# Second weight pair rescaled two slots later, queries of two head pairs in one buffer, operand places and load order of the weights changed

## The chip, the cores and the metric

One core of one Trainium2 chip runs the whole program. The metric is device time in microseconds, the median of several executions. Each of them is one launch of a fused chain: pooled attention, a gated feed-forward layer, and a second gated feed-forward layer.

## The reference

```
k_p, v_p = mean of k, v over each 8 rows                  # 8 x 8 heads, 576 rows -> 72, 64 wide
a = softmax(q k_p^T / 8) v_p                              # x: [4608, 512]
h = x @ w_in;  g = h * clip(h + 3, 0, 6) / 6;  y = g @ w_out          # d_ff 2048
out = (silu(y @ w_gate) * (y @ w_val)) @ w_out2                       # d_ff 1536
```

All of it is float32. The kernel keeps float32 accuracy with float32r matmuls in threes: each operand is split into a high and a low part, and high*high, high*low and low*high are added up in PSUM. The weights come as raw 64-bit words and are converted to float32 on the chip.

## The kernel before, in words

The kernel has three stages, one after the other.

**First stage: attention and the first up-projection.** The 4608 rows are cut into NB = 9 blocks of N = 512. For block j, 16 up-projections (`up`, line 623: 12 matmuls of 512 columns each) run on TensorE, while the attention steps of block j + 1 are woven between them (`attn_slot`). A planner sorts the attention steps of all units by hand-set lags (`when`, `when_startup`); each engine executes its instructions in that order. A block's rows belong to one batch or to two, so that each head pair gives a *segment* of n rows per batch. Block 0 has n = 512, block 1 has 64 and 448, block 2 has 128 and 384, then 192/320, 256/256, 320/192, 384/128, 448/64, and 512 again. A segment's queries are fetched by four DMAs on SP's queue (line 384), 128 bytes a packet, into one of three buffers `q_in`; a VectorE transpose (line 485) turns them into `qT` for the scores (line 503). A load is issued 12 steps after the transpose of the third segment before it.

Beside this, in blocks 1 to 8 a *prep* converts the other weights. The list `prep_at` gives each of 26 preps its slots: a prep starts every 6 slots (one slot is one up-projection) and, from the 21st prep on, every 8 slots of the second stage. Its steps: fetch the first pair of quarters (slot 0) and the second pair (slot 1) into `wstg`; rescale both pairs on ScalarE (slot 3, line 135); join the 64-bit words of each pair on VectorE (slots 4 and 5, lines 141 and 144); sums (slot 7, on GpSimd, line 207 and 212); split into high and low part (slots 8 to 10); store to DRAM (slots 10 and 11).

**Second stage: the first down-projection**, in 9 blocks of 256-column products by Winograd's form of Strassen's scheme: 7 products per block (`down_b`, line 902), each of four chunks c = 0..3 of 12 matmuls, in the order c = 0, 1, 2, 3. The stationary operand is the weight chunk `pw`, the moving one the split activation `gb`. The weights of all seven products are fetched once from DRAM: those of products 0 to 2 late in the first stage, those of products 3 to 6 in a row right after its last stores of `g` (line 642), 16 loads of 512 KB (line 868).

**Third stage: the second layer**, in six groups p of 768 rows: 24 up-products in units of 7 (`up2`: P1, P6, P5, P2, P4, P7, P3, six matmuls of 384 columns each) and 7 down-products (`down2`, 54 matmuls of 256 columns each), all by line 716.

**Operand places.** Three tables shift where an operand starts inside its buffer, in 4-byte words: `P1_AT` for the four weight chunks of product 0 in the second stage (all other `pw` chunks start at multiples of 1024 in their buffers); `GC_AT` for the split activations of single chunks (n, c) in `down2`; and `X_AT` for the operands of `up2`, by name, with 8 where nothing is given.

All DMAs of these stages are issued by SP's queue in program order.

Of the kernel before, what the change touches and what calls it, by code (L numbers as in the profile page):

```python
# [23 lines left out]
def kernel(  # L24
# [27 lines left out]
    nc = tc.nc  # L52
# [174 lines left out]
    PREP_A = 20  # L227
    for u in range(len(preps)):
        first = 6 * u if u < PREP_A else F1 * (NB - 1) + 6 + 8 * (u - PREP_A)
        for step, off in enumerate((0, 3, 4, 5, 7, 8, 9, 9, 10, 10, 11, 1)):  # L230
            prep_at.setdefault(first + off, []).append((u, step))

    def prep_slot(n):
# [4 lines left out]
    def prep_step(u, step):  # L238
        kind, f, m = preps[u]
        if step in (0, 11):  # L240
            place = A7 if kind == "up" else B7
            pairs = (("11", "21"), ("12", "22")) if kind == "up" else (("11", "21"), ("22", "12"))
            for pair in pairs[step == 11:][:1]:
                t = stg_p.tile([P, WC, 2], F32, tag="stg", name="wstg")
                for i, quarter in enumerate(pair):
                    r, c = int(quarter[0]) - 1, int(quarter[1]) - 1
                    if kind == "up":
                        w = (w_gate, w_val)[m].bitcast(I32).rearrange("(k p) f -> p k f", p=P)
                        src = w[:, 2 * c:2 * c + 2, 2 * P * (2 * f + r):2 * P * (2 * f + r + 1)]
                    else:  # L250
                        row = P * (2 * f + r if kind == "dn" else NP1 * r + f)
                        w = (w_out2 if kind == "dn" else w_out).bitcast(I32)[row:row + P, :]
                        src = w[:, 4 * P * c:4 * P * (c + 1)]
                    fetch_into(t[:, WH * i:WH * (i + 1)], src)
                a, b = (place[quarter] for quarter in pair)
                prep_t.setdefault(("q", u), []).append((t, slice(a, b + 1, b - a)))
        elif step == 1:
            for s, _ in prep_t["q", u]:
                rescale(s)
        elif step in (2, 3):  # L260
            if step == 2:
                prep_t["f", u] = f32(new_q7("q7")).rearrange("p (s n) -> p s n", s=8)
            s, at = prep_t["q", u].pop(0)
            join(s, prep_t["f", u][:, at].bitcast(I32), 2)
        elif step == 4:
            q, eng = prep_t["f", u], nc.gpsimd if u < PREP_A else nc.vector
            if kind == "up":
                sums_a(eng, lambda n: q[:, A7[n]])
            else:
                sums_b(eng, lambda n: q[:, B7[n]])  # L270
        elif step in (5, 6):
            if step == 5:
                prep_t["s", u] = new_s7("s7").rearrange("p (s a n) -> p s a n", s=7, a=2)
            q, t, part = prep_t["f", u], prep_t["s", u], slice(0, 4) if step == 5 else slice(4, 7)
            nc.scalar.copy(out=t[:, part, 0], in_=q[:, part])
        elif step in (7, 8):
            q, t, part = prep_t["f", u], prep_t["s", u], slice(0, 4) if step == 7 else slice(4, 7)
            nc.vector.tensor_tensor(out=t[:, part, 1], in0=q[:, part], in1=f32(t[:, part, 0]), op=ALU.subtract)
        else:
            part = slice(0, 4) if step == 9 else slice(4, 7)  # L280
            t = prep_t["s", u][:, part]
            if kind == "up":
                nc.sync.dma_start(
                    out=s_up[f][m][:, part].rearrange("p s a k f -> p (s a k f)"),
                    in_=f32(t).rearrange("p s a f -> p (s a f)"),
                )
            else:
                nc.sync.dma_start(out=(s_dn if kind == "dn" else s_w1)[:, part, f], in_=f32(t))
# [23 lines left out]
    sync4 = [nc.sync] * 4  # L312

    def load_k(b, p, eng):
        t = a_p.tile([SP_, 2, POOL, D], F32, tag="k", name="k_in", bufs=2)
# [55 lines left out]
                    )  # L371
            vt_t[0, p] = vt[p // 2][:96, p % 2]

    def load_q(seg, engines):
        t = a_p.tile([P, N // 32, 32], F32, tag="q", name="q_in", bufs=3)
        fetch_q(t, seg, engines)
        q_t[seg] = t

    def fetch_q(t, seg, engines):
        b, p, s0, n = seg  # L380
        for h2 in range(2):
            for dh in range(2):
                p0 = 64 * h2 + 32 * dh
                engines[2 * h2 + dh].dma_start(  # L384
                    out=t[p0:p0 + 32, :n // 32],
                    in_=q[b, 2 * p + h2, s0:s0 + n, 32 * dh:32 * dh + 32]
                    .rearrange("(c s) d -> s c d", s=32),
                )

    def reduce_k(b, p):  # L390
        kp = a_p.tile([SP_, 2, D], F32, tag="kp", name="kp", bufs=2)
# [79 lines left out]
            op0=ALU.mult, op1=ALU.subtract,  # L471
        )

    def prep_q(seg):
        n = seg[3]
        t = a_p.tile([P, N // 32, 32], F32, tag="qT", name="qT", bufs=2)
        if seg in segs[:KT]:

            s, ps = q_t.pop(seg), psum("k", [P, QJ, P])
            for j in range(QJ):  # L480
                nc.tensor.transpose(out=ps[:, j], in_=s[:, j].rearrange("p h d -> p (h d)"), identity=ident)
            qT_t[seg] = t.rearrange("p c s -> p (c s)")
            nc.vector.tensor_copy(out=qT_t[seg].rearrange("d (p j) -> d j p", j=QJ), in_=ps)
            return
        nc.vector.transpose(out=t[:, :n // 32], in_=q_t.pop(seg)[:, :n // 32])  # L485
        qT_t[seg] = t.rearrange("p c s -> p (c s)")

    n_unit = [0]
    s_t, ps_t, x_ps, x_e, n_exp = {}, {}, {}, {}, [0]
# [173 lines left out]
            nc.sync.dma_start(out=t[:, 2 * r + c], in_=y_d[:, 2 * r:2 * r + 2, t0:t0 + M])  # L663
        ys[p] = t

    GC_AT = {(0, 0): 16, (3, 0): 56, (4, 0): 16}
    X_AT = {'21': 24, 'T3': 16}

    def x_step(p, n, lo_eng, sum_eng):

# [9 lines left out]
        a = X_AT.get(what, 8)  # L680
        x = xc[p, what] = x[:, a:a + 4 * M].rearrange("p (a k n) -> p a k n", a=2, k=2)
        split(x[:, 0], x[:, 1], v(what), lo_eng)
        if then:
# [171 lines left out]
            t = gq[j, slot] = lb["gq"].tile([P, NP1, MB], F32, tag=f"gq{slot}", name="gq")  # L855
            nc.sync.dma_start(out=t, in_=g_d[j][:, r, c])

    P1_AT = (16, 1088, 2168, 3216)

    def new_pw(n, t):  # L860
        k = BIG // NCB
        at = P1_AT if n == 0 else [k * c for c in range(NCB)]
        lb["pw", DN[n][2]] = [t[:, a:a + k].rearrange("p (f a n) -> p f a n", f=CB, a=2) for a in at]

    def load_pw(n, half):
        what = DN[n][2]
        for c in range(NCB // 2 * half, NCB // 2 * (half + 1)):
# [40 lines left out]
    def evac_b(j, n):  # L908
# [35 lines left out]
        elif what == "P3":  # L944
# [6 lines left out]
    units, unit_end, segs, heads = [], [], [], []  # L951
    seg_of, first_in_seg, first_in_head = {}, {}, {}
    for j in range(NB):
        t0 = j * N
        while t0 < (j + 1) * N:
# [5 lines left out]
            for p in range(KT):  # L961
                seg = (b, p, s0, n)
                at_unit = len(units) if alone or p % 2 == 0 else len(units) - 1
                first_in_seg.setdefault(at_unit, []).append(len(segs))
                segs.append(seg)
                if s0 == 0:
                    first_in_head.setdefault(at_unit, []).append(len(heads))
# [54 lines left out]


    at = {st: n for n, st in enumerate(steps)}
    seg_no = {sg: n for n, sg in enumerate(segs)}
    head_no = {hd: n for n, hd in enumerate(heads)}
    rings = {}

# [5 lines left out]

    for i, u in enumerate(units):
        before(*((what, i) for what in "SXANMEFTULVWY"))
    for i, sg in ((i, seg_no[s]) for i, u in enumerate(units) for s in seg_of[u]):
# [14 lines left out]
    for i, u in enumerate(units):  # L1052
# [17 lines left out]
    for sg, s in enumerate(segs):  # L1070
        ring("qT", 2, ("P", sg), ("S", max(i for i, u in enumerate(units) if s in seg_of[u])))
# [19 lines left out]
    def do_step(st):  # L1091
# [17 lines left out]
        elif what == "Q":  # L1109
            split_v_lo(*heads[i])  # L1110
        elif what == "P":
            prep_q(segs[i])
            for n in (range(KT, KT + 3) if i == KT - 1 else (i + 3,)):
                if KT <= n < len(segs) and i >= KT - 1:
                    later.append((done[0] + 12, lambda n=n: load_q(segs[n], sync4)))
        elif what == "S":
            scores(units[i])
        elif what == "N":
# [37 lines left out]
    with tc.manual_schedule():  # L1156
# [64 lines left out]
        for j in range(NB):  # L1221
            for f in range(F1):
                if (j, f) == (NB - 1, 0):
                    attn_ctx.close()
                    for nm in ("px", "gq"):
                        lb[nm] = right_b.enter_context(
                            tc.tile_pool(name=nm, bufs=1, side="right", reuse_waits="tile"))
                    new_pw(0, lb["px"].tile([P, 4296], F32R, tag="px", name="pw"))
# [26 lines left out]
        l1.close()  # L1255
        l1_ps.close()
        lb["o"] = left_b.enter_context(tc.tile_pool(name="ob", bufs=1, reuse_waits="tile"))
# [96 lines left out]
```

## Time and profile before

| | us |
|---|---|
| median of 3 runs (1733.76 to 1734.01) | 1733.95 |
| the profiled execution | 1737.34 |
| its span, first to last instruction | 1735.4 |
| TensorE busy (matmul) | 1685.9 |
| VectorE busy | 1334.3 |
| ScalarE busy | 752.0 |
| GpSimd busy | 642.4 |

The profiled execution took 1.94 us more than its span and 3.39 us more than the median of the runs. Shares of busy time are means over three stages that have different limits, and are to be read stage by stage. PE is TensorE, PEld its weight loads, DVE VectorE, ACT ScalarE, POOL GpSimd; "SPq" rows are DMAs that SP issues.

### The profile page before, as it was taken

How to read it: one execution, taken by the hardware profiler on the slowest of the kernel's cores; microseconds unless marked ns; L12 is line 12 of the kernel's file. 1: busy time of each engine (PE TensorE's matmuls, PEld its weight loads, DVE VectorE, ACT ScalarE, POOL GpSimd, SP SyncE). 2: the span in 40 equal slices, each digit the busy share in tenths (PEclk: the TensorE clock that was granted, in tenths of full speed). 3: DMA queues.
4: the chain of work that ended last, by engine and by line, in shares of the span. 5: the costliest groups of instructions: out<-in, count | busy, mean ns of one | idle time of the engine just before them, and what ended most of it. 6: DMA issues, size and time to landing. Idle time of an engine off the chain costs nothing.

```text
span 1735.4 us, 30785 instructions
## 1 busy us (share of the span) xinstructions
PE 1685.9 (97%) x11116; PEld 1591.3 (92%) x11116; DVE 1334.3 (77%) x2356; ACT 752.0 (43%) x1656; POOL 642.4 (37%) x821
## 2 busy tenths in 40 slices
PE   5889999999999999999999999999999999999999
PEld 4678887878788899999999999999999999999998
DVE  6797897888975678988898668668668668668666
ACT  6565554555554445545554224224224224224223
POOL 6555676666822000000000550550550560560560
PEclk9799999999999999999999999999999999999999
DMA  7666897888767975655655878878878878878776
GB/s 185 171 178 185 245 272 247 254 268 250 227 229 257 411 312 177 194 206 220 216 198 186 288 242 295 294 242 296 294 241 296 296 242 295 297 243 290 268 243 219
DMA packets 239801, 432.49 MB, mean 249 GB/s; under 512 B 87328, under 2 KB 169248, under 8 KB 224288
## 3 DMA queue, kind: packets, MB, share of 16 engines
q1 hardware_dynamic: 238592, 430.25, 75.2%
q8 instruction: 88, 1.44, 0.3%
q14 instruction: 65, 0.53, 0.1%
q10 hardware_dynamic: 1056, 0.26, 0.1%
HBM read 326.11 MB, written 104.33 MB: 248 GB/s over the span
## 4 chain that ended last, share of the span: by engine, by line
PE 80%; DMA 9%; DVE 7%; SPq 2%; issue 1%; ACT 1%; POOL 0%; DVEq 0%; ACTq 0%; POOLq 0%
PE b L716 45%; PE b L902 18%; PE h L623 13%; DMA q_in<-in_q_dram 2%; DMA g<-g 1%; DMA gq<-g 1%; PE pss L503 1%; SPq L384 1%; DVE g L638 1%; DMA wstg<-in_moe_w_in_dram 1%; DMA sup<-s 1%; DMA qv<-in_q_dram 1%; DVE qT L485 1%; DMA pw<-sw 1%; DVE vtl L469 1%
## 5 line engine op out<-in xcount | busy, mean ns | idle before, releaser
L716 PE MATMUL b<-xc,wr 128*128 128x384 f32 x3024 | 529.9, 336 | 3.0 <-ACT xc L149 2.7
L716 PEld LDWEIGHTS b<-xc,wr 128*128 128x128 f32 x3024 | 528.0, 189 | 3.7 <-ACT xc L149 3.0
L623 PE MATMUL h<-x,wu 128*128 128x512 f32 x1728 | 432.3, 402 | 5.5 <-DVE g L638 5.5
L763 POOL TENSOR_TENSOR s<-s,c 128x384 f32<-128x384 f32 x144 | 143.0, 1018 | 740.4 <-ACT s L761 740.2
L725 DVE TENSOR_TENSOR c<-c,b 128x384 f32<-128x384 f32 x504 | 265.4, 552 | 177.0 <-PE b L716 147.6
L623 PEld LDWEIGHTS h<-x,wu 128*128 128x128 f32 x1728 | 322.0, 192 | 71.2 <-DVE g L638 6.6
L902 PE MATMUL b<-gb,pw 128*128 128x256 f32 x3024 | 348.4, 277 | 0.1
L902 PEld LDWEIGHTS b<-gb,pw 128*128 128x128 f32 x3024 | 347.6, 188 | 1.0 <-DVE gb L150 0.9
L716 PE MATMUL b<-wr,gc 128*128 128x256 f32 x2268 | 260.1, 277 | 0.0
L716 PEld LDWEIGHTS b<-wr,gc 128*128 128x128 f32 x2268 | 259.9, 188 | 0.0
L149 ACT CAST gb<-gq 128x512 fp32r<-128x512 f32 x252 | 154.3, 621 | 148.2 <-PE b L902 104.6
L150 DVE TENSOR_TENSOR gb<-gq,gb 128x512 fp32r<-128x512 f32 x252 | 166.3, 687 | 46.1 <-ACT gb L149 45.2
L770 POOL TENSOR_TENSOR gf<-s,c 128x384 f32<-128x384 f32 x144 | 168.2, 1194 | 67.1 <-DVE c L725 64.8
L149 ACT CAST gc<-gf 128x768 fp32r<-128x768 f32 x126 | 105.7, 839 | 184.1 <-POOL gf L770 101.2
L761 ACT ACTIVATE s<-c 128x384 f32<-128x384 f32 x144 | 73.5, 526 | 199.6 <-DVE c L725 198.2
L150 DVE TENSOR_TENSOR gc<-gf,gc 128x768 fp32r<-128x768 f32 x126 | 133.6, 1093 | 14.8 <-ACT gc L149 13.0
L634 ACT ACTIVATE g<-h,half 128x512 f32<-128x512 f32 x144 | 99.1, 688 | 77.1 <-PE h L623 65.7
L638 DVE SCALAR_TENSOR_TENSOR g<-g,h 128x512 f32<-128x512 f32 x144 | 97.5, 677 | 22.2 <-ACT g L634 22.2
L551 POOL TENSOR_TENSOR e<-e,sm 128x288 f32<-128x288 f32 (+4 forms) x74 | 48.4, 654 | 124.5 <-DVE sm L547 107.4
L733 ACT COPY c<-b 128x384 f32<-128x384 f32 x72 | 34.0, 472 | 125.5 <-PE b L716 125.5
L880 DVE TENSOR_TENSOR gq<-gq 128x1024 f32<-128x1024 f32 x72 | 87.7, 1219 | 0.0
L207 DVE TENSOR_TENSOR gf<-gf 128x768 f32<-128x768 f32 (+1 forms) x66 | 66.9, 1029 | 12.1 <-POOL gf L770 10.9
(101 smaller groups left out, 1660.9 us busy)
## 6 DMA issues: line engine op xcount, KB each, us to landing
wr<-sup SPq DMA_DIRECT2D x72, 1024.0 KB
wr<-sdn SPq DMA_DIRECT2D x84, 768.0 KB
wr<-sup SPq DMA_DIRECT2D x72, 768.0 KB
g<-g SPq DMA_DIRECT2D x144, 256.0 KB
gq<-g SPq DMA_DIRECT2D x36, 1024.0 KB
wstg<-in_moe_w_out_dram SPq DMA_DIRECT2D x56, 256.0 KB
pw<-sw SPq DMA_DIRECT2D x28, 512.0 KB
sup<-s SPq DMA_DIRECT2D x12, 1024.0 KB
```

The source lines that it names most:

```text
L149: nc.scalar.copy(out=hi, in_=src)
L150: lo_engine.tensor_tensor(out=lo, in0=src, in1=f32(hi), op=ALU.subtract)
L623: nc.tensor.matmul(out=ps, lhsT=w(kt, wh), rhs=x(kt, xh), start=first and n == 0, stop=last and n == 3 * len(kts) - 1,)
L634: nc.scalar.activation(out=t, in_=ps, func=ACTF.Relu, bias=half, scale=1.0 / 6.0)
L638: nc.vector.scalar_tensor_tensor(out=t, in0=t, scalar=1.0, in1=ps, op0=ALU.min, op1=ALU.mult)
L716: nc.tensor.matmul(out=ps, lhsT=w(wh), rhs=x(xh), start=first and n == 0, stop=last and n == 2)
L725: add = lambda dst, a, b: nc.vector.tensor_tensor(out=dst, in0=a, in1=b, op=ALU.add)
L761: nc.scalar.activation(out=g[q], in_=c[q], func=ACTF.Sigmoid)
L763: nc.gpsimd.tensor_tensor(out=g[q], in0=g[q], in1=c[q], op=ALU.mult)
L770: nc.gpsimd.tensor_tensor(out=gf[p][:, GP[TURN[q]], f], in0=g[q], in1=c[q], op=ALU.mult)
L880: nc.vector.tensor_tensor(out=v(what), in0=v(a), in1=v(b), op=op)
L902: nc.tensor.matmul(out=ps[:, d], lhsT=w[c][:, k, wh, P * d:P * (d + 1)], rhs=g[:, gh, k], start=what == place and (c, d, k, m) == (0, 0, 0 ...
```

## The change

Five edits, none of which alters what is computed.

1. A prep's step 1 rescales only the first pair, in slot 3; a new step 12 rescales the second pair in slot 5, and the second join moves from slot 5 to slot 6.
2. Segments of at most 256 rows share a buffer: the queries of two head pairs are fetched by eight DMAs in a row into one `q_in`, and one VectorE transpose serves both. A load is then issued 12 steps after the transpose of the third *group* before it.
3. `P1_AT`, `GC_AT` and `X_AT` change. In `P1_AT` the chunks 1 to 3 now start at multiples of 64 words, and chunk 0 stays 16 words off. `GC_AT` loses (3, 0). `X_AT` is given for groups p = 0 and 1 alone; from p = 2 on all operands start at 8.
4. Chunk 0 of product 3's weights gets a tile of its own, `lead`, behind the output tiles `ob` of the second stage, which are taken beforehand to fix its place.
5. The order of the 16 late weight loads changes: first chunks 1, 2, 3 of product 3, then the four chunks of product 4, then chunk 0 of product 3, then products 5 and 6.

```diff
-        for step, off in enumerate((0, 3, 4, 5, 7, 8, 9, 9, 10, 10, 11, 1)):
+        for step, off in enumerate((0, 3, 4, 6, 7, 8, 9, 9, 10, 10, 11, 1, 5)):
...
-        elif step == 1:
-            for s, _ in prep_t["q", u]:
-                rescale(s)
+        elif step in (1, 12):
+            rescale(prep_t["q", u][0][0])
...
+    def load_q(group):
         t = a_p.tile([P, N // 32, 32], F32, tag="q", name="q_in", bufs=3)
+        for i, (b, p, s0, n) in enumerate(group):
+            for h2 in range(2):
+                for dh in range(2):
+                    p0, c0 = 64 * h2 + 32 * dh, i * n // 32
+                    nc.sync.dma_start(
+                        out=t[p0:p0 + 32, c0:c0 + n // 32],
...
-        nc.vector.transpose(out=t[:, :n // 32], in_=q_t.pop(seg)[:, :n // 32])
-        qT_t[seg] = t.rearrange("p c s -> p (c s)")
+        m = n * len(group) // 32
+        nc.vector.transpose(out=t[:, :m], in_=q_t.pop(seg)[:, :m])
...
-    GC_AT = {(0, 0): 16, (3, 0): 56, (4, 0): 16}
-    X_AT = {'21': 24, 'T3': 16}
+    GC_AT = {(0, 0): 16, (4, 0): 16}
+    X_AT = {(0, "T1"): 56, (0, "T4"): 40, (0, "22"): 0, (1, "T1"): 32, (1, "T4"): 48}
...
-    P1_AT = (16, 1088, 2168, 3216)
+    P1_AT = (16, 1088, 2112, 3136)
+    LEAD = 3
...
-                first_in_seg.setdefault(at_unit, []).append(len(segs))
+                if n > N // 2 or p % 2 == 0:
+                    first_in_seg.setdefault(at_unit, []).append(len(loads))
+                    loads.append([])
+                loads[-1].append(seg)
...
         new_pw(6, big_x("pw"))
-        for n in (3, 4, 5, 6):
+        load_pw(LEAD, 0, (1, 2, 3))
+        l1.close()
+        l1_ps.close()
+        for nm in ("o", "lead"):
+            stack = left_b if nm == "o" else right_b
+            lb[nm] = stack.enter_context(tc.tile_pool(name=nm + "b", bufs=1, reuse_waits="tile"))
+            if nm == "o":
+                for tag in ("o12", "o11", "o21", "o22"):
+                    lb["o"].tile([P, 2, MB], F32, tag=tag, name=tag)
+        lead = lb["lead"].tile([P, BIG // NCB], F32R, tag="lead", name="pw")
+        lb["pw", DN[LEAD][2]][0] = lead.rearrange("p (f a n) -> p f a n", f=CB, a=2)
+        load_pw(LEAD + 1, 0)
+        load_pw(LEAD + 1, 1)
+        load_pw(LEAD, 0, (0,))
+        for n in (5, 6):
             for h in range(2):
                 load_pw(n, h)
```

## Rows read from the trace of the kernel before

**Rows 1.** Busy time by stretch: us, then PE, PEld, DVE, ACT, POOL, clock, DMA
```profile
0.00:125.00 125.00, 91.16 (x438) 72.81 (x439) 98.41 (x222) 76.65 (x307) 71.97 (x131) 0.89 0.70 178
125.00:591.00 466.00, 457.70 (x2362) 383.22 (x2361) 369.15 (x830) 243.08 (x628) 259.31 (x403) 0.99 0.80 252
591.00:940.00 349.00, 348.85 (x3029) 348.00 (x3028) 304.54 (x432) 184.43 (x305) 0.00 (x0) 1.00 0.62 223
940.00:951.00 11.00, 8.04 (x29) 7.32 (x28) 9.07 (x13) 4.79 (x6) 0.00 (x0) 0.69 0.57 192
951.00:1735.40 784.40, 780.11 (x5266) 779.91 (x5264) 553.15 (x864) 243.06 (x412) 311.16 (x288) 1.00 0.80 271
```

**Rows 2.** Timeline, 272 to 296 us: start, us, instruction, idle before and its releaser
```profile
277.55 0.82 SPq L123 DMA_DIRECT2D wstg<-in_moe_w_out_dram  x2
...
283.69 0.68 ACT L135 ACTIVATE wstg<-wstg 128x512 f32<-128x512 f32 x1 [5.11 <-DMA wstg<-in_moe_w_out_dram]
...
290.56 4.62 PE L623 MATMUL h<-x,wu 128*128 128x512 f32 x12 [2.85 <-DVE g L638]
```

**Rows 3.** Chain of waits in order of time: start, us, what
```profile
296.49 2.77 PE h L623 x12
...
347.29 3.21 DMA wstg<-in_moe_w_val_dram
350.58 0.68 ACT wstg L135
```

**Rows 4.** Timeline of TensorE, 362 to 366 us
```profile
364.08 2.12 PE L623 MATMUL h<-x,wu 128*128 128x512 f32 x8 [1.24 <-DVE g L638]
```

**Rows 5.** Timeline of SP's issues, 20 to 46 us
```profile
20.65 11.20 SPq L384 DMA_DIRECT2D q_in<-in_q_dram  x12
...
34.95 0.39 SPq L123 DMA_DIRECT2D wstg<-in_moe_w_in_dram  x1
...
41.02 3.78 SPq L384 DMA_DIRECT2D q_in<-in_q_dram  x8
```

**Rows 6.** Timeline of VectorE, 38 to 48 us
```profile
44.05 0.24 DVE L485 STREAM_TRANSPOSE qT<-q_in 128x64 f32<-128x64 f32 x1 [3.41 <-DMA q_in<-in_q_dram]
```

**Rows 7.** Timeline of SP's issues, 584 to 606 us and 606.5 to 607.5 us
```profile
598.68 7.52 SPq L868 DMA_DIRECT2D pw<-sw  x7
...
606.54 0.32 SPq L868 DMA_DIRECT2D pw<-sw  x1
```

**Rows 8.** Chain of waits, 590 to 630 us
```profile
592.07 9.52 DMA pw<-sw
```

**Rows 9.** DMA, 590 to 630 us: packets and rate
```profile
DMA packets 5389, 16.49 MB, mean 412 GB/s; under 512 B 498, under 2 KB 2290, under 8 KB 4978
```

**Rows 10.** TensorE by stretch: us, busy (instructions touching it), clock, DMA share, GB/s
```profile
608.64:610.05 1.41, 1.41 (x14) 1.00 1.02 418
708.12:713.80 5.68, 5.68 (x50) 1.00 0.93 326
713.80:719.24 5.44, 5.44 (x50) 1.00 0.15 56
763.79:769.44 5.65, 5.65 (x50) 1.00 0.40 121
708.12:709.56 1.44, 1.44 (x14) 1.00 0.94 358
709.56:710.93 1.37, 1.37 (x14) 1.00 0.96 372
```

**Rows 11.** TensorE by stretch, third stage
```profile
1367.78:1368.82 1.04, 1.04 (x7) 1.00 1.06 382
1367.78:1375.08 7.30, 7.30 (x43) 1.00 0.99 365
1438.52:1444.65 6.13, 6.13 (x56) 1.00 0.77 254
1444.65:1450.88 6.23, 6.23 (x56) 1.00 0.64 230
```

More of the change, by code (lines that the diff above doesn't have):

```diff
@@ L311 @@
     vm_t, vt_t, es_t = {}, {}, []
-    sync4 = [nc.sync] * 4
     def load_k(b, p, eng):
@@ L372, in load_first @@
             vt_t[0, p] = vt[p // 2][:96, p % 2]
-    def load_q(seg, engines):
+    def load_q(group):
         t = a_p.tile([P, N // 32, 32], F32, tag="q", name="q_in", bufs=3)
[L376 to L388, printed above, removed]
+        for i, (b, p, s0, n) in enumerate(group):
[4 more added lines that the diff above has]
+                        out=t[p0:p0 + 32, c0:c0 + n // 32],
+                        in_=q[b, 2 * p + h2, s0:s0 + n, 32 * dh:32 * dh + 32]
+                        .rearrange("(c s) d -> s c d", s=32),
+                    )
+        q_t[group[0]] = t
     def reduce_k(b, p):
@@ L472, in split_v_lo, with prep_q @@
         )
-    def prep_q(seg):
-        n = seg[3]
+    def prep_q(group):
+        seg, n = group[0], group[0][3]
         t = a_p.tile([P, N // 32, 32], F32, tag="qT", name="qT", bufs=2)
@@ L484, in prep_q @@
             return
-        nc.vector.transpose(out=t[:, :n // 32], in_=q_t.pop(seg)[:, :n // 32])
-        qT_t[seg] = t.rearrange("p c s -> p (c s)")
+        m = n * len(group) // 32
+        nc.vector.transpose(out=t[:, :m], in_=q_t.pop(seg)[:, :m])
+        for i, seg in enumerate(group):
+            qT_t[seg] = t.rearrange("p c s -> p (c s)")[:, n * i:n * (i + 1)]
     n_unit = [0]
@@ L679, in x_step @@
             x = pool.tile([P, 4 * M + 64], F32R, tag="x" + what, name="xc")
-        a = X_AT.get(what, 8)
+        a = X_AT.get((p, what), 8)
         x = xc[p, what] = x[:, a:a + 4 * M].rearrange("p (a k n) -> p a k n", a=2, k=2)
@@ L863, in new_pw, with load_pw @@
         lb["pw", DN[n][2]] = [t[:, a:a + k].rearrange("p (f a n) -> p f a n", f=CB, a=2) for a in at]
-    def load_pw(n, half):
+    def load_pw(n, half, cs=None):
         what = DN[n][2]
-        for c in range(NCB // 2 * half, NCB // 2 * (half + 1)):
+        for c in cs or range(NCB // 2 * half, NCB // 2 * (half + 1)):
             nc.sync.dma_start(
@@ L950 @@
            512: ([(256, 128), (256, 128)], 0)}
-    units, unit_end, segs, heads = [], [], [], []
+    units, unit_end, segs, heads, loads = [], [], [], [], []
     seg_of, first_in_seg, first_in_head = {}, {}, {}
@@ L1024 @@
     at = {st: n for n, st in enumerate(steps)}
-    seg_no = {sg: n for n, sg in enumerate(segs)}
+    load_no = {sg: n for n, group in enumerate(loads) for sg in group}
     head_no = {hd: n for n, hd in enumerate(heads)}
@@ L1036 @@
         before(*((what, i) for what in "SXANMEFTULVWY"))
-    for i, sg in ((i, seg_no[s]) for i, u in enumerate(units) for s in seg_of[u]):
+    for i, sg in ((i, load_no[s]) for i, u in enumerate(units) for s in seg_of[u]):
         before(("P", sg), ("S", i))
@@ L1069 @@
         ring("aT", 2, ("U", i), ("V", i))
-    for sg, s in enumerate(segs):
-        ring("qT", 2, ("P", sg), ("S", max(i for i, u in enumerate(units) if s in seg_of[u])))
+    for sg, group in enumerate(loads):
+        ring("qT", 2, ("P", sg), ("S", max(i for i, u in enumerate(units) if set(group) & set(seg_of[u]))))
     for h in range(len(heads)):
@@ L1111, in do_step @@
         elif what == "P":
-            prep_q(segs[i])
+            prep_q(loads[i])
             for n in (range(KT, KT + 3) if i == KT - 1 else (i + 3,)):
-                if KT <= n < len(segs) and i >= KT - 1:
-                    later.append((done[0] + 12, lambda n=n: load_q(segs[n], sync4)))
+                if KT <= n < len(loads) and i >= KT - 1:
+                    later.append((done[0] + 12, lambda n=n: load_q(loads[n])))
         elif what == "S":
@@ L1227 @@
                             tc.tile_pool(name=nm, bufs=1, side="right", reuse_waits="tile"))
-                    new_pw(0, lb["px"].tile([P, 4296], F32R, tag="px", name="pw"))
+                    new_pw(0, lb["px"].tile([P, 4168], F32R, tag="px", name="pw"))
                     new_pw(1, big_x("pw"))
@@ L1251 @@
         new_pw(6, big_x("pw"))
-        for n in (3, 4, 5, 6):
+        load_pw(LEAD, 0, (1, 2, 3))
[13 more added lines that the diff above has]
+        for n in (5, 6):
             for h in range(2):
                 load_pw(n, h)
-        l1.close()
-        l1_ps.close()
-        lb["o"] = left_b.enter_context(tc.tile_pool(name="ob", bufs=1, reuse_waits="tile"))
         l2["ps"] = ctx.enter_context(tc.tile_pool(name="ps2", bufs=8, space=PSUM, reuse_waits="tile"))
```

## The prediction

> **What bounds the kernel now.** I read the stages first, then the chain of waits, then the places where TensorE (PE) stands idle. By stage [rows 1]: from 591 to 940 us and from 951 us to the end PE has work all the time (348.85 of 349.00 us, and 780.11 of 784.40 us, where the rest is the tail). There only the rate of the matmuls counts, and whatever stops PE is paid in full. From 125 to 591 us PE is busy for 457.70 of 466.00 us, so 8.3 us of waits are left there. In the first 125 us it is busy for 91.16 us: start-up, a relay of loads, ScalarE and VectorE. So the change has four places where it can act: start-up, the waits of the first stage, the start of the second stage, and the matmul rate of stages two and three.
>
> **Rescale moved, part 1.** At 277.55 us SP issues the second pair's fetch; ScalarE, whose queue is in order, stands from 278.6 us on before that pair's rescale and gets it only at 283.69, after 5.11 us of idling [rows 2]. Behind it in ScalarE's queue lie the activation of the up-projection and the copies of the attention. PE runs dry: the 12 matmuls at 290.56 us begin after 2.85 us of idling and take 4.62 us, against 2.77 us for an ordinary dozen [rows 2, 3], as the clock was lowered. That event costs 2.85 + 1.85 = 4.7 us. A second one runs from a fetch at 347.29 us by the rescale at 350.58 us, and the chain leads on from there over VectorE to a wait of PE of 1.24 us at 364.08 us [rows 3, 4]. One slot of the first stage is 466.00 / 128 = 3.64 us [rows 1], so two slots later means 7.3 us more for the fetch, against waits of 5.11 us and less. Both events should go: 5.9 us. What is late next is the first pair, whose rescale stays three slots (10.9 us) behind its fetch, and the sums on GpSimd in slot 7, for which the second join is now one slot ahead and not two. The step issues no more work: two rescales, two joins, as before; in slots 3 and 5 ScalarE and VectorE have one piece less or one piece later. I count 5.0 us of gain, between 7 (all of it and one of the other waits) and a loss of 2 (the bursts below make new waits).
>
> **Queries in pairs, part 2.** Sixteen of the 32 transposes of short segments go; one that remains is twice as wide. The shortest takes 0.24 us [rows 6], so by that 16 of them are some 4 us of VectorE at most, nearly all beside PE's matmuls: counted at nothing. The DMAs are as many as before, but eight in a row, and they reach further ahead. At start-up this cuts both ways. VectorE now waits 3.41 us for the queries of the fourth short segment [rows 6], which in the new order come with the first burst; that wait goes. But the burst of 12 at 20.65 us, which SP took 11.20 us to issue [rows 5], becomes one of 20. At 3.78 / 8 = 0.47 us each, as the eight at 41.02 us took, or 11.20 / 12 = 0.93 us, as that burst took [rows 5], the eight more put 4 to 7 us ahead of the weight fetch at 34.95 us [rows 5], and the rescale of that weight holds ScalarE up by about as long as VectorE is freed. I take a loss of 0.5 us over the start-up and block 0, between a gain of 3.4 (the wait alone) and a loss of 5.
>
> **Operand places, part 3.** In the second stage a product of 48 matmuls takes 5.44 us in the good case and 5.68 us as product 0; of product 0's chunks the first, 16 words off a multiple of 64, takes 1.44 us, the second, on such a multiple, 1.37 us [rows 10]. With chunks 2 and 3 on multiples of 64 product 0 should take 5.44 + 0.07 = 5.51 us: 0.17 us less, in nine blocks 1.5 us. After a wait of PE the slower rate can stay: in block 4 product 3 takes 5.65 us at places where others take 5.44 [rows 10]; products 4 to 6 of block 4, and 3 to 6 of block 0, run like it. From the code, `lead` starts 16 words off too (between the weight pool and the output tiles lie 28,688 words, 16 over a multiple of 64), so it is a second chunk of the kind that resets the rate: four products (3 to 6) in each of two blocks gain 0.21 us, 1.7 us in all, and nine blocks pay 0.07 us each, 0.6 us. In the third stage a `down2` product of 6.23 us is followed or preceded by 6.13 us without the shifted chunk (3, 0) [rows 11]: 0.1 us in six groups, 0.6 us. A unit of `up2` takes 7.30 us where seven times its first product would be 7.28 [rows 11]: 0.02 us in 48 units of groups 2 to 5, 1.0 us. Groups 0 and 1 get five places that no row shows; the spread of known places is 6 ns a matmul (1.44 against 1.37 us for 12), so 5 x 72 x 6 ns = 2.2 us either way; I take nothing. Sum of part 3: a gain of 4.2 us, between 1 and 7.
>
> The Trainium skill speaks against this part: "SBUF — State Buffer", section "Who interferes with whom", says that TensorE has one read port for the moving operand and one for the weights, independent of each other, and never waits on anyone. By that no place would matter, the whole 4.2 us would be nothing and the sum below that much higher. The rows of 1.44 and 1.37 us for the same 12 matmuls differ from it, at a full clock.
>
> **The order of the late weight loads, parts 4 and 5.** Here I see the largest single term. Chunk 0 of product 3 was the first of 16 loads of 512 KB, and becomes the eighth; but product 3 still begins with chunk 0. The DMA engines are saturated there (412 GB/s, share over 1 [rows 9, 10]), so each place further back costs a load's time. The first load is issued at 598.68 us, the eighth at 606.54 [rows 7]; such a load landed 9.52 us after its issue [rows 8]. The old chunk 0 so lands at about 608.2 us, and product 3 starts at 608.64 us with no wait [rows 10]: just in time. In the new order chunk 0 lands at 606.54 + 9.5 = 616.1 us, while PE comes to it at about 608.5 us (0.17 us sooner by product 0). That is a wait of 7.6 us; by the rate (seven loads of 524,288 bytes at 412 GB/s are 8.9 us) it is 8.5. I take 8.0. Nothing hides it: PE's queue is in order, and stages two and three have no idle time in which to win it back. The chunks of product 4 have landed by then, and the loads behind come during the wait. After idling of 2.85 us PE lost 1.85 us to a lowered clock; in the 11 us after 940 us, where it idled again, the granted clock was 0.69, that is 3.4 us lost [rows 1, 2]. I add 2.4 us, between 1.8 and 3.4. Together a loss of 10.4 us, between 9.4 and 12.3. The output tiles taken beforehand hold no instruction and cost nothing; if the wait for their memory were carried to the first output copy twice, it would fall inside the same idle time.
>
> **The sum.** - 5.0 + 0.5 - 4.2 + 10.4 = + 1.7 us, against the profiled execution's 1737.34 us 1739.0 us, and against the median of 1733.95 us 1735.7 us; I name 1735.7 us. Ends of the single terms put together by half their widths give 1731 to 1740 us for this case.
>
> **The rivals.** (a) *First-stage waits only change places* (slower). The bursts of eight query loads push a weight fetch of the first pair back by 4 us, ScalarE stands before the first rescale as it does now before the second, and the 5.9 us come back elsewhere: 1735.7 + 5.0 = about 1741 us. For it: SP issues without a pause in that stretch, and the fetch at 277.55 us landed 6 us later [rows 2]. Against it: three slots are 10.9 us. It decides as soon as the first fetch is issued more than 5 us later than now. (b) *The eighth load is in time* (faster). If the loads before it land sooner than I think, or PE comes to product 3 later, the wait is gone: 1735.7 - 10.4 = about 1725 us. Against it: a saturated stretch of 412 GB/s, and the old chunk 0 with less than half a microsecond to spare. (c) *The first stage gains more*: the 8.3 us of waits between 125 and 591 us shrink by six more at start-up and there, with the load wait as forecast: 1730 us. (d) *Places mean nothing*, as the skill's rule has it: 1735.7 + 4.2 = 1739.9 us; for it speaks no row, against it those of part 3.
>
> **How the numbers follow.** Forecast 0.47, (a) 0.23, (b) 0.14, (c) 0.12, (d) 0.04. What a measurement of this kernel can tell from no change is 0.2%, 3.5 us: faster is below 1730.5, slower above 1737.4. Of the forecast's share 0.04 falls below, 0.31 within and 0.12 above; (a) and (d) count as slower, but 0.03 of (a) as within; (b) is faster, and of (c) 0.07. Faster 0.25, within 0.39, slower 0.36. The range reaches from just above (b) to just above (a): 1727 to 1743 us; the forecast's own is 1731 to 1740 us.
>
> **What would show it.** Part 1: no idling of ScalarE before line 135, and dozens of 2.77 us around 290 us. Part 2: no wait of the transpose for `q_in` before 50 us, the weight fetch of 34.95 us issued some 4 us later. Part 3: product 0 at 5.51 us, product 3 of every block at 5.51 us, no product at 5.65 us after it, `up2` units at 7.28 us. Part 5: PE idle for about 8 us before product 3 of block 0, some 17 us into the second stage, and a lowered clock behind it. If that idle time is missing, the prediction is wrong by 10 us to the fast side; if the first stage has as many waits as now, by 5 us to the slow side.

## The result and the profile after

| | us |
|---|---|
| before, median of 9 runs beside the changed kernel | 1733.76 (1729.99 to 1739.51) |
| changed, median of 9 runs | 1742.91 (1738.14 to 1751.33) |
| ratio changed / before, 95% interval | 1.0052 [1.0036, 1.0069] |
| the changed kernel's profiled execution, its span | 1743.29, 1741.5 |

The change costs 0.52%, some 9 us. That is inside the range of 1727 to 1743 us by 0.1 us only, and it is not the likeliest case: "within 0.2%" had the largest chance, and the time is that of rival (a) or a little over it. That the range still holds is luck: its upper end was set by rival (a), whose path the runs below bear out only in part.

The stages of the changed kernel (us, then PE, PEld, DVE, ACT, POOL, clock, DMA share, GB/s), to be read against [rows 1]:

```profile
0.00:125.00 125.00, 91.21 (x444) 73.66 (x445) 100.65 (x220) 77.40 (x308) 74.72 (x132) 0.90 0.73 180
125.00:591.50 466.50, 456.76 (x2358) 381.70 (x2357) 364.93 (x816) 242.50 (x626) 253.41 (x402) 0.99 0.80 253
591.50:948.00 356.50, 349.37 (x3025) 348.78 (x3024) 304.14 (x432) 185.27 (x305) 0.00 (x0) 0.99 0.61 216
948.00:959.00 11.00, 7.79 (x35) 7.22 (x34) 9.06 (x12) 4.79 (x6) 0.00 (x0) 0.84 0.66 203
959.00:1741.50 782.50, 778.15 (x5261) 777.95 (x5259) 553.22 (x864) 242.93 (x412) 311.12 (x288) 1.00 0.80 272
```

The first stage ends at 591.5 us as before: nothing of the expected gain is left there. The second stage takes 356.5 us instead of 349.0. The third, from its pause at 948 us to the end of the span, takes 793.5 us against 795.4.

What makes the second stage longer stands in the changed kernel's chain of waits, its timeline of TensorE and its stretch behind the wait:

```profile
605.65 10.13 DMA pw<-sw
```

```profile
615.91 9.30 PE L900 MATMUL b<-gb,pw 128*128 128x256 f32 x54 [7.12 <-DMA pw<-sw]
```

```profile
612.00:624.00 12.00, 8.09 (x46) 8.12 (x47) 1.55 (x3) 1.86 (x3) 0.00 (x0) 0.59 1.00 400
```

PE stands for 7.12 us before product 3's chunk 0, which is issued as the eighth load and lands 10.13 us later. Over the last stretch, which begins 3.9 us before the wait ends, the granted clock is 0.59; over the 8.44 us of product 3 alone (615.91 to 624.35 us) it is 0.64.

In the first stage the stall of [rows 2] is gone. In the changed kernel's timeline the dozens at that place run in about 3 us, with no idling before them:

```profile
285.83 3.02 PE L620 MATMUL h<-x,wu 128*128 128x512 f32 x12
...
289.99 2.90 PE L620 MATMUL h<-x,wu 128*128 128x512 f32 x12
```

In its place stands another wait, on GpSimd, with what hangs on it (timeline, GpSimd and TensorE of the changed kernel):

```profile
383.67 2.06 POOL L395 TENSOR_TENSOR k_in<-k_in 72x512 f32<-72x512 f32 x2 [3.22 <-DMA k_in<-in_k_dram]
385.81 0.45 POOL L395 TENSOR_TENSOR kp<-k_in 72x128 f32<-72x128 f32 x1
386.22 0.25 POOL L563 TENSOR_TENSOR et<-e,et 128x32 f32<-128x32 f32 x1
```

```profile
386.52 0.66 PE L574 MATMUL pst<-ident,et 128*96 128x128 f32 x2 [2.43 <-POOL et L563]
...
387.53 4.08 PE L620 MATMUL h<-x,wu 128*128 128x512 f32 x12
```

GpSimd's queue is in order: it waits for a key load, sums the keys (line 395), and only then writes `et`, for which PE's transposes wait. The next dozen takes 4.08 us. The whole first stage after 50 us of the changed kernel, waits of GpSimd and of PE (us in total, times, longest):

```profile
POOL k_in L395 <- DMA k_in<-in_k_dram: 28.9, 8, 7.1
```

```profile
PE pst L574 <- POOL et L563: 7.3, 4, 2.7
```

In the kernel before these are 0.9 us in 2 times and 1.6 us in one.

### The profile page after: what moved, and what is told of

The parts are those of the page before. It is cut to its first block, busy times and chain, and to the rows that moved or that the text cites. A ratio compares the mean times of both kernels' runs of the same rounds, so it can differ in the third digit from the quotient of the medians.

```text
span 1741.5 us, 30726 instructions
## 1 busy us (share of the span) xinstructions
PE 1683.3 (97%) x11116; PEld 1589.3 (91%) x11116; DVE 1332.0 (76%) x2340; ACT 752.9 (43%) x1656; POOL 639.2 (37%) x821
## 4 chain that ended last, share of the span: by engine, by line
PE 81%; DMA 7%; DVE 6%; POOL 2%; ACT 1%; issue 1%; SPq 1%; DVEq 0%; POOLq 0%; ACTq 0%
PE b L713 45%; PE b L900 19%; PE h L620 14%; DMA k_in<-in_k_dram 2%; DMA pw<-sw 1%; PE pss L500 1%; DMA g<-g 1%; DMA wstg<-in_moe_w_in_dram 1%; DMA q_in<-in_q_dram 1%; DVE g L635 1%; DVE vtl L464 1%; POOL k_in L395 1%; PE pst L574 1%; DVE s L277 1%; DVE mx L510 1%
## 5 line engine op out<-in xcount | busy, mean ns | idle before, releaser
L900 PEld LDWEIGHTS b<-gb,pw 128*128 128x128 f32 x3024 | 349.0, 189 | 7.8 <-issue 7.3
L150 DVE TENSOR_TENSOR gc<-gf,gc 128x768 fp32r<-128x768 f32 x126 | 134.1, 1095 | 14.5 <-ACT gc L149 12.9
L207 DVE TENSOR_TENSOR gf<-gf 128x768 f32<-128x768 f32 (+1 forms) x66 | 66.9, 1029 | 12.1 <-POOL gf L767 10.9
```

The lines of the kernel that those rows point to most:

```text
L150: lo_engine.tensor_tensor(out=lo, in0=src, in1=f32(hi), op=ALU.subtract)
L900: nc.tensor.matmul(out=ps[:, d], lhsT=w[c][:, k, wh, P * d:P * (d + 1)], rhs=g[:, gh, k], start=what == place and (c, d, k, m) == (0, 0, 0 ...
```

## The experiments

Each was timed beside the kernel before, whose median was 1733.4 us beside e1 to e4, 1734.9 us beside e5, e9, e10 and e11, and 1734.7 us beside e6, e8, e12 and e13. Single runs of one kernel lie 4 to 14 us apart, and the profiled execution is one of them. The last three columns come from the profiled execution, 50 to 600 us, in us: the longest wait of ScalarE's rescale (line 135) for its weight fetch, GpSimd's waits for key loads, and PE's waits for GpSimd's `et`.

| kernel | median us | ratio to before | rescale | keys | `et` |
|---|---|---|---|---|---|
| before | | 1 | 5.1 | 0.9 | 1.6 |
| e2 load order only | 1745.75 | 1.0072 [1.0055, 1.0089] | 3.6 | 0 | 1.6 |
| e5 places only | 1734.73 | 0.9993 [0.9980, 1.0006] | 4.5 | 3.0 | 1.6 |
| e4 pairs only | 1742.28 | 1.0054 [1.0035, 1.0073] | 8.4 | 11.6 | 1.6 |
| e10 pairs, two transposes | 1741.87 | 1.0036 [1.0024, 1.0048] | 8.9 | 14.0 | 1.6 |
| e9 pairs, two groups ahead | 1732.15 | 0.9990 [0.9976, 1.0004] | 5.2 | 12.4 | 1.8 |
| e3 rescale only | 1727.32 | 0.9965 [0.9951, 0.9978] | 0.6 | 2.7 | 1.3 |
| e11 rescale, places | 1725.58 | 0.9942 [0.9927, 0.9958] | 1.0 | 5.4 | 1.3 |
| e6 rescale, places, lead first | 1729.93 | 0.9976 [0.9965, 0.9987] | 1.2 | 9.5 | 1.3 |
| e8 rescale, places, pairs | 1736.41 | 1.0007 [0.9994, 1.0019] | 1.1 | 31.3 | 10.1 |
| e13 as e8, two groups ahead | 1733.06 | 0.9991 [0.9977, 1.0005] | 0.3 | 28.8 | 9.1 |
| e1 changed, lead first | 1738.93 | 1.0020 [1.0004, 1.0036] | 1.5 | 27.1 | 8.2 |
| e12 as e1, two groups ahead | 1735.89 | 1.0005 [0.9995, 1.0015] | 0.9 | 21.2 | 7.5 |
| changed | 1742.91 | 1.0052 [1.0036, 1.0069] | 1.1 | 28.9 | 7.3 |

**The load order alone** (e2): the kernel before, with the late loads reordered and no tile of its own for the chunk.

```diff
...
-        for n in (3, 4, 5, 6):
+        load_pw(3, 0, (1, 2, 3))
+        load_pw(4, 0)
+        load_pw(4, 1)
+        load_pw(3, 0, (0,))
+        for n in (5, 6):
```

> The kernel before with only the order of the late weight loads changed (chunk 0 of product 3 behind product 4, in its old place in memory). Theory: the load order alone costs 10.3 us, whatever the place: 1733.8 + 10.3 = 1744.1 us, PE idle some 7.4 us before product 3 of block 0. Rival (the lead tile's own memory, not the order, makes the wait): no change against before, 1733.8.

Measured 12.4 us over the kernel before. The wait is there, TensorE's timeline:

```profile
614.38 10.90 PE L902 MATMUL b<-gb,pw 128*128 128x256 f32 x70 [7.61 <-DMA pw<-sw]
```

So the order costs its 10 us, and a little more, by itself, without the lead-in.

**The lead-in with its chunk loaded first** (e1): the changed kernel, the order of the loads undone and the tile kept.

```diff
-        load_pw(LEAD, 0, (1, 2, 3))
...
-        load_pw(LEAD + 1, 0)
-        load_pw(LEAD + 1, 1)
-        load_pw(LEAD, 0, (0,))
-        for n in (5, 6):
+        load_pw(LEAD, 0, (0, 1, 2, 3))
+        for n in (4, 5, 6):
```

> The changed kernel with chunk 0 of product 3 loaded first of the 16 late weight loads again (lead tile kept); nothing else differs. Theory (the eighth place in the queue costs a wait of 7.1 to 7.4 us and 2.9 us of lowered clock): 10 us less than the changed kernel's 1742.9, so about 1732.6, no wait of PE for pw, product 3 of block 0 at 5.52 us, and products 4 to 6 of block 0 at 5.44 us. Rival (PE would wait for something else there, such as the activation split, once the load is early): a wait of several us stays before product 3 and the time stays above 1738.

A miss: by the medians only 4.0 us came back, by the ratios 5.5 us. The wait for the weights is gone, but the sixteen loads start late. SP's issues, first in e1, then in e2:

```profile
593.41 3.03 SPq L639 DMA_DIRECT2D g<-g  x3
602.31 12.93 SPq L866 DMA_DIRECT2D pw<-sw  x16
```

```profile
593.41 3.02 SPq L642 DMA_DIRECT2D g<-g  x3
596.98 17.60 SPq L868 DMA_DIRECT2D pw<-sw  x16
```

SP's own wait in e1 (us in total, times, longest), and what came of it on ScalarE and then on PE:

```profile
SPq L866 <- DMA g<-g: 6.2, 2, 5.8
```

```profile
629.41 2.18 ACT L149 CAST gb<-gq 128x512 fp32r<-128x512 f32 x4 [4.99 <-DMA gq<-g]
```

```profile
630.08 0.38 PE L900 MATMUL b<-gb,pw 128*128 128x256 f32 x1 [1.42 <-ACT gb L149]
```

The new tile lies in memory that the first stage frees only when its last store of `g` has landed. SP stands before that one load, and the fifteen behind it and the gate loads behind them all come 5.3 us later. So the changed order keeps SP from standing there, and moves the wait to PE. The Trainium skill, "DMA: Bandwidth & Descriptors", section "Anatomy of one DMA — SWDGE (gpsimd) path", says that DMA engines do not wait on semaphores and that the issuing sequencer does so before dispatch. It says so in a section on GpSimd's path; the 5.8 us of SP, another issuer, agree.

This accounts for a part of the miss only. In the profiled executions the second stage, from its first matmul to the end of its last, takes 349.7 us in e1 and 356.7 us in the changed kernel, so that 7.0 of the 10 us came back there; of the rest the late gate load takes some 2 us (product 6 of block 0 at 7.02 us and product 0 of block 1 at 6.23 us, where the changed kernel has 5.65 and 5.51 us). That the medians give back less than this profile is not explained: e1's twelve runs lie between 1732.2 and 1740.8 us, and the profiled one took 1734.3 us.

**The moved rescale alone** (e3): the kernel before with the first two hunks of the diff, of which the first is shown.

```diff
-        for step, off in enumerate((0, 3, 4, 5, 7, 8, 9, 9, 10, 10, 11, 1)):
+        for step, off in enumerate((0, 3, 4, 6, 7, 8, 9, 9, 10, 10, 11, 1, 5)):
...
```

> The kernel before with only the second pair's rescale and join moved. Theory of the forecast: the waits of ScalarE before line 135 go, and with them up to 5.9 us of waits of PE in the first stage: 1728 to 1731 us. Rival (the waits only change places, as in the changed kernel, whose first stage ends at the same 591.5 us): within 2 us of before, 1732 to 1736, with other waits of PE (transposes for the POOL or DVE tail) in the first stage.

It gains 6 us, as that theory has it (the median lies 0.7 us below its range); the longest wait of a rescale falls from 5.1 to 0.6 us.

**The query pairs alone** (e4): the grouping of loads and transposes on the kernel before.

```diff
...
+                if n > N // 2 or p % 2 == 0:
+                    first_in_seg.setdefault(at_unit, []).append(len(loads))
+                    loads.append([])
+                loads[-1].append(seg)
```

> The kernel before with only the queries of two head pairs in one buffer and one transpose. Theory: bursts of eight query loads hold SP's queue and the work behind it up, so that the first stage gets longer by 2 to 4 us: 1736 to 1738. Rival (the wait for q_in at start-up goes and VectorE has 4 us less to do): 1730 to 1733.

They lose 8.9 us. PE's order of instructions in the first stage is that of the kernel before, so the start of each matmul can be set against the same one there. Of the differences one stands out, 6.4 us at once, in block 2. TensorE's and ScalarE's timelines of e4 there:

```profile
245.52 0.38 PE L420 MATMUL psk<-ident,kp 72*128 72x72 f32 x1 [6.25 <-ACT kbd L431]
```

```profile
244.15 0.65 ACT L135 ACTIVATE wstg<-wstg 128x512 f32<-128x512 f32 x1 [8.40 <-DMA wstg<-in_moe_w_out_dram]
```

PE waits for ScalarE's `kbd`, and ScalarE stands 8.40 us before a rescale, with `kbd` behind it in its queue. It is the stall of [rows 2] again, in another block and larger. The fetch that it waits for, in SP's issues of e4 and of the kernel before:

```profile
237.46 1.06 SPq L123 DMA_DIRECT2D wstg<-in_moe_w_out_dram  x2
```

```profile
231.31 1.05 SPq L123 DMA_DIRECT2D wstg<-in_moe_w_out_dram  x2
```

It is issued 6.15 us later, behind a burst of eight query loads. The two profiled executions differ by 3.2 us in all (1740.53 against 1737.34), and so by less than the medians: the trace shows where one large wait comes from, not the whole of the 8.9 us.

**Pairs, fetched two groups ahead** (e9) and **pairs, with two transposes** (e10), each on e4:

```diff
-            for n in (range(KT, KT + 3) if i == KT - 1 else (i + 3,)):
+            for n in (range(KT, KT + 2) if i == KT - 1 else (i + 2,)):
```

```diff
-        m = n * len(group) // 32
-        nc.vector.transpose(out=t[:, :m], in_=q_t.pop(seg)[:, :m])
+        src, m = q_t.pop(seg), n // 32
+        for i in range(len(group)):
+            nc.vector.transpose(out=t[:, m * i:m * (i + 1)], in_=src[:, m * i:m * (i + 1)])
```

> The kernel before with the query pairs alone, but each group of loads fetched two groups ahead instead of three. Theory Q (queue): the pairs cost their 8.9 us because SP's queue carries the query loads earlier and eight at a time, so that the key loads behind them land later and GpSimd, which sums the keys, waits for them (11.6 us in 3 waits in the run of the pairs alone, of which one of 8.3 us held up TensorE by 6.3). Two groups ahead: no such wait over 2 us, the first stage ends at 590 to 593 us, 1733 to 1736 in all. Theory V (VectorE): the one long transpose for two head pairs holds up what is behind it on VectorE; it is still there, so 1742 as with the pairs alone.

> The kernel before with the query pairs alone, loads as in the changed kernel, but with one transpose for each of the two head pairs instead of one for both. Theory Q: loads and their order are the same, so GpSimd waits for the keys as before and the time stays at 1742 (1739 to 1744). Theory V: the loss goes, 1733 to 1735.

The queue was the right suspect: with the groups fetched nearer the loss goes (1732.2 us), with two transposes most of it stays (1741.9 us). But it was the wrong load. Theory Q named the key loads and expected no key wait over 2 us in e9; 12.4 us of them are left, the longest 5.5 us, and in neither kernel did they add to PE's `et` waits (1.6 and 1.8 us, against 1.6 before). What fell is the wait of the rescale, in ScalarE's timeline first of e10, then of e9:

```profile
244.67 0.65 ACT L135 ACTIVATE wstg<-wstg 128x512 f32<-128x512 f32 x1 [8.91 <-DMA wstg<-in_moe_w_out_dram]
```

```profile
241.51 0.65 ACT L135 ACTIVATE wstg<-wstg 128x512 f32<-128x512 f32 x1 [5.20 <-DMA wstg<-in_moe_w_out_dram]
```

PE's wait there is 6.70 us in e10 and 2.53 us in e9. These 4 us are the largest single difference between the two, and less than half of the 9.7 us between their medians; the rest was not traced to its waits.

**The operand places alone** (e5): the three tables of the diff on the kernel before. As in the changed kernel, the tile of product 0's weights shrinks with them, from 4296 to 4168 words.

```diff
+    P1_AT = (16, 1088, 2112, 3136)
+    GC_AT = {(0, 0): 16, (4, 0): 16}
+    X_AT = {(0, "T1"): 56, (0, "T4"): 40, (0, "22"): 0, (1, "T1"): 32, (1, "T4"): 48}
...
```

> The kernel before with the new operand places alone (P1_AT, GC_AT, X_AT). The theory (a matmul's rate goes with the place of its operand): product 0 of every block at 5.51 to 5.52 us instead of 5.68 (9 x 0.16 = 1.4 us), the third stage 2.0 us shorter as in the changed kernel, so 3.4 us below the kernel before: about 1730. The rival, that places mean nothing and that the changed kernel's shorter products came with its order: product 0 stays at 5.68, no difference to the kernel before (1733.4).

A miss in the medians. In its profile product 0 takes 5.51 and 5.52 us in blocks 2 to 8, as expected; but blocks 0 and 1 ran at the slower rate of 5.65 us after a wait, and its first stage, whose code is that of the kernel before, ended 2.2 us later. From profile to profile the first stage of one code differs by several us: the first matmul of the second stage, in e3 and then in e11, which have the same first stage:

```profile
585.67 4.51 PE L901 MATMUL b<-gb,pw 128*128 128x256 f32 x37
```

```profile
579.84 5.79 PE L901 MATMUL b<-gb,pw 128*128 128x256 f32 x49
```

A part of 2 us is hard to see through that.

**Rescale and places** (e11), on the kernel before, nothing else.

> The two parts that should pay, on the kernel before: the second pair of weights rescaled two slots later and the new operand places; no query pairs, no second lead-in, loads of the weights in the order of before. The theory (the parts add up): 1727.3 with the moved rescale alone, less 3.4 for the places: about 1724. Rival: the gain of the moved rescale in the first stage is eaten by a later wait as it is in the changed kernel, 1730.

1725.6 us, near the theory's 1724: faster than both kernels, by 0.58% than the one before.

**Without the lead-in** (e8): the changed kernel with the load order and the place of before.

```diff
-        load_pw(LEAD, 0, (1, 2, 3))
...
+        for n in (3, 4, 5, 6):
+            for h in range(2):
+                load_pw(n, h)
```

> The changed kernel without its second lead-in: the late weight loads in the order of before, product 3's first chunk in its old place; moved rescale, query pairs and operand places stay. If the lead-in's only effect is the late load (7.3 us of waiting and 2.9 us of lowered clock behind it in the changed kernel), 10.2 us come back: 1742.9 - 10.2 = 1732.7, product 3 of block 0 at about 5.5 us. Rival: the lead-in also pays for itself by setting the rate of the later products in each block, so that without it products fall to 5.65 us in several blocks: 1736 to 1738.

In between: 6.5 us came back, product 3 of block 0 takes 5.44 us; and in blocks 3 and 4 eleven products run at about 5.65 us, as the rival has it. But e1, which has the tile, shows such products in blocks 3 and 4 as well (eight of 5.65 to 5.68 us), and the changed kernel does not; that the tile sets the rate is not shown.

**All but the lead-in, two groups ahead** (e13): e8 with e9's edit.

> As the kernel without the lead-in, and the query groups fetched two ahead instead of three: moved rescale, query pairs, operand places, with both losses taken out. If the losses are the late weight load and the query loads ahead of the key loads, nothing else: 1725 to 1727, as with the moved rescale and the places alone (1725.6). Rival: one transpose for two head pairs costs something by itself, which shows only once the rescale stands later: 1729 to 1732.

A miss, 6 to 8 us too high. The rescale waits 0.3 us at most now, but the key waits are 28.8 us, and here they reach PE. The SP queue between the same pair of weight fetches and the second key load behind it, in e11 and then in e13:

```profile
425.11 1.16 SPq L123 DMA_DIRECT2D wstg<-in_moe_w_val_dram  x2
426.33 1.96 SPq L383 DMA_DIRECT2D q_in<-in_q_dram  x4
428.38 1.18 SPq L641 DMA_DIRECT2D g<-g  x2
429.66 0.55 SPq L315 DMA_DIRECT2D k_in<-in_k_dram  x1
430.30 0.51 SPq L641 DMA_DIRECT2D g<-g  x1
430.86 2.02 SPq L383 DMA_DIRECT2D q_in<-in_q_dram  x4
432.99 0.36 SPq L282 DMA_DIRECT2D sup<-s  x1
433.45 0.35 SPq L315 DMA_DIRECT2D k_in<-in_k_dram  x1
```

```profile
428.63 1.12 SPq L123 DMA_DIRECT2D wstg<-in_moe_w_val_dram  x2
429.80 4.62 SPq L378 DMA_DIRECT2D q_in<-in_q_dram  x8
434.52 1.18 SPq L639 DMA_DIRECT2D g<-g  x2
435.80 0.55 SPq L314 DMA_DIRECT2D k_in<-in_k_dram  x1
436.44 0.51 SPq L639 DMA_DIRECT2D g<-g  x1
437.00 4.98 SPq L378 DMA_DIRECT2D q_in<-in_q_dram  x8
442.09 0.36 SPq L282 DMA_DIRECT2D sup<-s  x1
442.55 0.35 SPq L314 DMA_DIRECT2D k_in<-in_k_dram  x1
```

It is the same sequence with eight for four. The second key load is issued 8.34 us behind the weights in e11 and 13.92 us in e13. In e11 GpSimd takes up those keys at 439.32 us without a wait; in e13 it waits 5.35 us, and PE then stands for `et`, which is still behind those keys in GpSimd's queue:

```profile
448.39 2.06 POOL L395 TENSOR_TENSOR k_in<-k_in 72x512 f32<-72x512 f32 x2 [5.35 <-DMA k_in<-in_k_dram]
```

```profile
451.24 0.66 PE L574 MATMUL pst<-ident,et 128*96 128x128 f32 x2 [3.94 <-POOL et L563]
```

The rival, that the one transpose costs something once the rescale stands later, has the nearer time and was not tried: e10 had the old rescale. The traces speak for the keys. PE's order of instructions is the same in e8 and in e11; at the first matmul of the second stage e8 is 13.2 us behind. Five jumps of 1.2 to 3.4 us, 10.9 us together, stand each at a transpose that waits for GpSimd's `et`; one such transpose gives 1.5 us back. PE's waits for VectorE are 9.9 us in e11 and 10.0 us in e8; in e13 they are 12.9 us, so that there some 3 us may be of another kind.

**Without the pairs** (e6: e1 with each segment a group of its own) and **all mended** (e12: e1 with e9's edit):

```diff
-                if n > N // 2 or p % 2 == 0:
+                if True:
```

> Moved rescale, operand places and the second lead-in with its chunk loaded first; no query pairs. Against the same without the lead-in (1725.6): if the lead-in is worth nothing or less, since its chunk waits for the last store of the first stage and holds up the loads behind it (in the earlier run with the lead loaded first the sixteen loads began 5.4 us later than in the run of the order alone and ScalarE waited 5.0 us for a gate load), 1727 to 1729. If it is worth having, 1722 to 1725.

> The changed kernel with both mended: product 3's first chunk loaded first, query groups fetched two ahead. Against the run without the lead-in and the groups two ahead: the same plus what the lead-in costs, 1727 to 1730; if the lead-in pays, 1722 to 1725.

The lead-in does not pay even with its chunk first: against the kernels without it, e6 stands 0.34% above e11, e12 0.14% above e13 and e1 0.13% above e8, that is 2 to 6 us. Only the first of these is clear of the intervals; in the profiled executions the second stage is 1.7 to 2.7 us longer with it in all three. e6 (1729.9 us) came out a little over its 1727 to 1729, and e12 6 us over its expectation, because that was built on e13's.

## Why the prediction was right and where it failed

Put up one on the other, the ratios give a sum: rescale and places - 0.58% (e11), the pairs on top + 0.65% (e8), the lead-in with its order on top + 0.45% (changed). In us, with 1734: - 10.0, + 11.3, + 7.8, together + 9.

- **Rescale moved, - 5.0.** Right. The stall of [rows 2] is gone in every kernel with the edit, no rescale waits over 1.5 us from 50 us on, and alone it brings 6 us (e3). That it shows nothing in the changed kernel is the pairs' doing.
- **Query pairs, + 0.5, between - 3.4 and + 5.** This is the step that failed. The prediction priced the burst at start-up alone; elsewhere it stands only in the lower bound of the rescale ("a loss of 2") and in rival (a). At start-up it was roughly right: no transpose waits for `q_in` there, the burst of 20 took 15.16 us, and the weight fetch of [rows 5] came at 39.63 us, 4.7 us later. But bursts of eight come back in every block with short segments, and behind them on SP's queue are the second weight fetch, for ScalarE, and the key loads, for GpSimd. With the rescale where it was, the late fetch costs most (rescale wait 8.4 us in e4). With the rescale moved that is cured, and the late keys take over: the `et` waits are 1.3 to 1.8 us wherever one of the two edits is missing, and 7.3 to 10.1 us in the five kernels that have both. "The DMAs are as many as before" was taken for a price of nothing; it is 0.54% alone and 0.65% with the rescale moved, 9 to 11 us, outside the bounds. That the key waits make up most of the second figure is read from traces (9.4 of the 13.2 us between the first stages of e11 and e8); no run took them away with the pairs kept.
- **Rival (a).** Its time was nearest, and its sentence came true: the waits of the first stage changed places and its end stayed at 591.5 us. Its path holds in part: bursts do push weight fetches back (4.7 us at start-up, 6.15 us in e4), but in the changed kernel no rescale waits over 1.1 us, and the keys and GpSimd stand where it named ScalarE.
- **Operand places, - 4.2.** Most single rows came as worked out, but the sum was too large. Windows of the changed kernel: product 0 and product 3 of block 2, then an `up2` unit of group 2:

```profile
679.53:685.05 5.52, 5.52 (x50) 5.52 (x49) 4.98 (x10) 2.48 (x4) 0.00 (x0) 1.00 0.85 279
695.93:701.45 5.52, 5.52 (x50) 5.52 (x49) 5.31 (x9) 2.49 (x4) 0.00 (x0) 1.00 0.47 172
```

```profile
1229.82:1237.10 7.28, 7.28 (x44) 7.28 (x43) 3.79 (x8) 1.20 (x3) 3.83 (x4) 1.00 0.77 255
```

  Product 0 gains 0.16 us, and product 3 pays 0.08 us in each block. In the third stage `down2` gains 0.1 us in each of six groups and the up-products of groups 2 to 5 gain 0.2 us each, but group 1 loses 0.3 us at its new places (87.9 against 87.6 us for its 24 up-products): from its first matmul to its last the stage takes 788.5 to 789.9 us in the kernels with the new places and 789.6 to 790.9 us in those without, some 1 us. By these rows the places bring some 2 us in the changed kernel, where 4.2 were forecast. The medians neither show nor exclude it: e5 stands 0.07% below the kernel before, with no change inside its interval, and e11 0.23% below e3, with intervals that overlap.

  The term that was too large is the 1.7 us of the second chunk that was to reset the rate. It did so in block 3 and did not in block 0; in e1 it was the other way round. After a product of 5.83 us and after the wait, in the changed kernel:

```profile
728.73:734.56 5.83, 5.83 (x50) 5.72 (x49) 5.65 (x9) 3.44 (x5) 0.00 (x0) 1.00 0.00 0
734.56:740.07 5.51, 5.51 (x50) 5.51 (x49) 5.12 (x7) 3.22 (x5) 0.00 (x0) 1.00 0.41 141
...
624.35:630.00 5.65, 5.65 (x51) 5.65 (x49) 3.53 (x6) 2.97 (x5) 0.00 (x0) 1.00 0.58 205
```

  In e11, without the lead-in, the same product of block 3 is followed by 5.65 us:

```profile
707.00:712.83 5.83, 5.83 (x51) 5.72 (x49) 5.65 (x9) 3.44 (x5) 0.00 (x0) 1.00 0.00 0
712.83:718.48 5.65, 5.65 (x50) 5.65 (x49) 5.25 (x8) 3.22 (x5) 0.00 (x0) 1.00 0.40 139
```

- **Places mean nothing (rival d).** The Trainium skill, "SBUF — State Buffer", section "Who interferes with whom", has TensorE with two independent read ports and waiting on no one. It speaks of engines that get in each other's way, and the prediction's step from there to places that mean nothing does not hold: the same 48 matmuls of product 0 take 5.52 us in the changed kernel and 5.68 us before [rows 10], at the same full clock. Why is not shown.
- **The order, + 10.4.** Right, and shown alone by e2 (+ 12.4 us in the medians): a wait of 7.12 us against 8.0 forecast, landing 10.13 us after issue against 9.52, and product 3 at 8.43 us behind it, 2.9 us over its 5.52, against 2.4 forecast. Undoing lead-in and order together gives back 6.5 us in the medians, not all of it.

So + 1.7 became + 9: 10.8 us from the pairs, less 2.6 us (the order and lead-in cost 7.8 on top of e8 and not 10.4) and 0.8 us (rescale and places brought 10.0 and not 9.2). The errors of the other terms took off a part of that of the pairs, which is the other half of the luck. Why the key waits double once the rescale is moved (11.6 to 14.0 us against 21.2 to 31.3) stays open, and a group's burst split into two fours was not tried.

## What to carry to other kernels

Price a burst of loads by what stands behind it on the issuing queue, in every block where it recurs: as many DMAs in a coarser order cost 9 to 11 us here, since a weight fetch and key loads, each awaited by an engine that takes its work in order, were behind. When two edits touch one stage, run each alone and both: the gain of the one was real and vanished in the other. A tile in memory that comes free late holds up its queue or its consumer, whichever meets it first; both orders of the lead-in lost.

## What the runs showed of the hardware that was not expected

The slower rate of a run of matmuls outlasts its cause. After one disturbed product of 5.83 us in block 3, products at unchanged places and full clock take 5.65 instead of 5.44 us, up to the end of their block in e11 (above) and through the whole next block in e8 and e13; a first chunk on another place ends that in one block and not in another. What decides it stays open.
